# Residue-major dilated turn, gated early loads, stores on two queues and a new order in an attention + feed-forward kernel

## The chip, the cores and the metric

One core of a Trainium2 chip. The runs were spread over four chips, each beside the kernel before on the same chip. The metric is device time in microseconds (us), as the median of several executions. In every run that lists both, the time is 1.6 to 1.8 us above the span of the same execution (from the first to the last instruction), so spans of profiles are compared with spans, and times with times.

In profile lines PE is TensorE, PEld its weight loads, DVE is VectorE, ACT ScalarE, POOL GpSimd and SP SyncE; a q after the name (SPq) marks the issue of a DMA. A line of a timeline gives the start in us, the duration, engine, source line, operation, shape and count, and in brackets how long the engine stood idle before and what ended that.

## The reference

Sliding-window attention over 8 batches of 8 heads, 576 tokens, head size 64, then a feed-forward block over its output:

```python
scores = scale * np.matmul(q, k.transpose(0, 1, 3, 2))
rel = pos[:, None] - pos[None, :]
mask_plain = (rel >= 0) & (rel < window)                                  # window = 32, heads 0 to 3
mask_dil = (rel >= 0) & (rel < window * dilation) & (rel % dilation == 0) # dilation = 4, heads 4 to 7
...                                   # softmax over the allowed keys, times v
h = x @ w_in                          # 4608 x 512 @ 512 x 2048
return np.maximum(0.01 * h, h) @ w_out
```

Dilated heads only look at keys of the same residue mod 4, so each residue is a plain window of 32 over 144 tokens.

## The kernel before

The work is cut into 16 half-batches n = 0 to 15 (even: the four plain heads, odd: the four dilated ones); each has three units of scores, u = 3n + s. "Batch 5" below means half-batch n = 5. A list of steps gives the order in which instructions are issued; each engine runs its own in that order. `S` is scores and exponential, `M` the mask product, `D` the values and the normalisation, `I` one group of four matmuls into the hidden layer (hp), `O` four of the 16 into the output (op), `Z` filler matmuls without use. `B` transposes on TensorE (n below 5), `T` by DMA (n from 5 on).

```python
NPE = 5
def qk_ap(x, n, pairs):
    ...
    if n >= NPE:
        return rows_ap(x, base, [[D, 96], [96 * D, 24], [1, D]])      # 256-byte pieces
def cast_qk(n, nm, eng, pairs=(0, 1)):    # fp32 -> fp16, two pieces of 96 x 768
def transpose(n):
    for nm, dst in (("q", qT), ("k", kT)):
        o = dst[n % NB][:, -2 * S:].rearrange("p (c r) -> p c r", r=96)
        nc.sync.dma_start_transpose(o, qkh[n, nm][0:96, :])
...
# in scores(u): dilated units read every fourth column
if kind:
    ka = kT[n % NB][r, tok - 128 + j: tok - 128 + j + 4 * kp - 3: 4]
    qa = qT[n % NB][r, tok - PAD + j: tok - PAD + j + 4 * w - 3: 4]
nc.tensor.matmul(sps[0:kp, hh, w * x:w * x + w], ka, qa, ...)
...
# in values(u): the normalisation, on ACT ("l") or on VectorE ("r")
if log_recip:
    nc.scalar.activation(out=ln, in_=den[:, 0:384], func=AF.Ln)
    nc.scalar.activation(out=rec, in_=ln, func=AF.Exp, scale=-1.0)
else:
    nc.vector.reciprocal(out=rec, in_=den[:, 0:384])
...
# in ff_out(t, g): after the last four of an output tile
if g == 3:
    ob = moe.tile([128, DM], FP32, tag="ob", bufs=2, name="ob")
    nc.scalar.copy(out=ob, in_=op)
    nc.scalar.dma_start(out[128 * t:128 * t + 128, :], ob)
```

The hidden groups, the output tiles, the transposes of `B` and some of the `D` units take their PSUM from one pool of four banks; ACT empties hp and op.

The softmax here doesn't subtract the row's maximum and nothing guards it: scores larger than these inputs give would overflow.

## Time and profile before

| | before |
|---|---|
| time, median | 324.41 us (324.23 to 324.82) |
| span of the first profile | 324.1 us, of an execution of 325.84 us |
| TensorE (PE) busy | 317.0 us, 98% |
| first hp group starts | 25.39 us |
| last matmul ends | 320.57 us |

A busy PE row says only that some matmul is in flight; fillers count and durations overlap. What can be added up is the distance from the start of a group to the start of the next one. The prediction below makes a price list of such distances and adds it up along the program. Four terms then make the span: the start of the first hp group, the priced work after it, the lag (how much later PE ends than start and price say; all its small waits), and the tail from PE's end to the end of the span.

### The profile page before, as it was taken

Reading aid. Unit: us, or ns where it says so; the run is one execution under the profiler, and the core shown is the slowest. Engines: PE = TensorE matmul, PEld = TensorE weight load, DVE = VectorE, ACT = ScalarE, POOL = GpSimd, SP = SyncE. Lnnn points to the kernel's source line nnn. Section 1 sums busy time; section 2 is a strip of 40 time slices with the busy share of each in tenths; the row PEclk is TensorE's granted clock in tenths of the full one; section 3 lists DMA queues with packets and bytes.
Section 4 is the critical chain, followed back from the end, with each engine's and each line's share of the span. In section 5 each row is a group of like instructions: output and inputs, shape, how many; then the busy total and the mean of one; then the engine's idle time right before and its main releaser. Section 6 shows DMA issues by size and latency. Waiting matters only on the chain.

```text
span 324.1 us, 6641 instructions
## 1 busy us (share of the span) xinstructions
PE 317.0 (98%) x2805; PEld 185.4 (57%) x2805; DVE 111.2 (34%) x166; ACT 191.8 (59%) x379; POOL 69.3 (21%) x92
## 2 busy tenths in 40 slices
PE   8998999999999999999999999999999999999995
PEld 3565585565756656656555565555665655565542
DVE  3473363203633084012353650454561530040000
ACT  1778696555756765936755773636856754464312
POOL 8751076033054220040310610200150000000000
PEclk9999999999999999999999999999999999999999
DMA  7999999969949931579899869303755000100003
GB/s 230 209 197 196 185 180 176 164 186 106 252 79 288 205 58 48 130 161 163 116 251 245 97 115 238 85 12 117 198 67 77 34 33 28 39 34 32 32 35 129
DMA packets 111198, 42.38 MB, mean 131 GB/s; under 512 B 96832, under 2 KB 105024, under 8 KB 111168
## 3 DMA queue, kind: packets, MB, share of 16 engines
q1 hardware_dynamic: 78240, 21.83, 34.2%
q0 software_dynamic: 27744, 10.68, 28.5%
q10 hardware_dynamic: 5184, 9.44, 7.9%
q8 instruction: 22, 0.36, 0.5%
q14 instruction: 8, 0.07, 0.1%
HBM read 36.70 MB, written 9.44 MB: 142 GB/s over the span
## 4 chain that ended last, share of the span: by engine, by line
PE 88%; DMA 9%; POOL 2%; ACT 0%; issue 0%; POOLq 0%
PE op L344 39%; PE hp L334 38%; DMA w<-in_moe_w_in_dram 5%; PE sps L261 5%; DMA vh<-in_v_dram 4%; PE den L287 3%; PE o L295 2%; PE tp L212 0%; POOL vh L169 0%; POOL vh L198 0%; POOL qh L183 0%; ACT ob L348 0%; POOL bias L106 0%; POOL bias L104 0%; POOL bias L103 0%
## 5 line engine op out<-in xcount | busy, mean ns | idle before, releaser
L334 PE MATMUL hp<-xT,w 128*128 128x384 f16 (+1 forms) x832 | 140.9, 315 | 0.7 <-DMA w<-in_moe_w_in_dram 0.7
L344 PE MATMUL op<-w,gt 128*128 128x512 f16 x576 | 137.0, 379 | 0.0
L336 ACT ACTIVATE gt<-hp 128x384 f16<-128x384 f32 (+1 forms) x208 | 93.0, 465 | 66.2 <-PE hp L334 63.8
L334 PEld LDWEIGHTS <-w 128*128 128x128 f16 x832 | 88.7, 114 | 43.9 <-issue 1.6
L344 PEld LDWEIGHTS <-gt 128*128 128x128 f16 x576 | 55.1, 98 | 57.2 <-issue 0.5
L312 DVE TENSOR_TENSOR xT<-o,rec 128x384 f16<-128x384 f32 (+1 forms) x64 | 33.6, 554 | 108.0 <-ACT rec L301 90.0
L303 DVE RECIPROCAL rec<-den 128x384 f32<-128x384 f32 x14 | 35.8, 2555 | 35.3 <-PE den L287 35.3
L264 ACT ACTIVATE er<-sps 128x768 f16<-128x768 f32 (+1 forms) x48 | 38.6, 804 | 10.7 <-PE sps L261 8.8
L348 ACT COPY ob<-op 128x512 f32<-128x512 f32 x36 | 21.1, 586 | 33.6 <-PE op L344 33.5
L186 POOL CAST kh<-kf 96x768 f16<-96x768 f32 x16 | 14.6, 936 | 106.3 <-DMA kf<-in_k_dram 81.2
L271 DVE TENSOR_TENSOR em<-er,mask 128x768 f16<-128x768 f16 (+1 forms) x44 | 25.4, 600 | 18.0 <-ACT er L264 17.8
L261 PE MATMUL sps<-qT,kT 64*128 64x96 f16 (+1 forms) x448 | 22.9, 229 | 0.0
L300 ACT ACTIVATE ln<-den 128x384 f32<-128x384 f32 x34 | 16.6, 488 | 8.7 <-PE den L287 8.1
L261 PEld LDWEIGHTS <-kT 64*128 64x128 f16 (+1 forms) x448 | 14.9, 121 | 10.2 <-issue 8.6
L301 ACT ACTIVATE rec<-ln 128x384 f32<-128x384 f32 x34 | 17.8, 524 | 1.1
L295 PEld LDWEIGHTS <-vh 128*64 128x64 f16 (+1 forms) x448 | 15.5, 110 | 2.4
L295 PE MATMUL o<-em,vh 128*64 128x96 f16 (+1 forms) x416 | 15.4, 201 | 0.0
L287 PE MATMUL den<-em,ones 128*64 128x384 f16 (+1 forms) x88 | 15.4, 346 | 0.0
L387 PE MATMUL wp<-xT 128*128 128x512 f16 x37 | 12.6, 455 | 1.5 <-DVE xT L113 1.3
L174 POOL DMA_DIRECT2D vh<-in_v_dram x16 | 10.0, 627 | 18.8 <-PE o L295 18.8
L195 POOL COPY vh<-vh 32x1472 f16<-32x1472 f16 x5 | 7.0, 1404 | 24.6 <-DMA vh<-in_v_dram 24.5
L287 PEld LDWEIGHTS <-ones 128*64 128x64 f16 (+1 forms) x96 | 5.3, 107 | 10.0 <-issue 8.3
(51 smaller groups left out, 97.8 us busy)
## 6 DMA issues: line engine op xcount, KB each, us to landing
out_dram<-ob ACTq DMA_DIRECT2D x36, 256.0 KB, 2.2
qf<-in_q_dram SPq DMA_DIRECT2D x11, 576.0 KB, 6.5
kf<-in_k_dram SPq DMA_DIRECT2D x11, 576.0 KB, 7.7
vh<-in_v_dram POOLq DMA_DIRECT2D x8, 288.0 KB, 7.5
w<-in_moe_w_in_dram POOLq DMA_DIRECT2D x4, 512.0 KB, 16.1
w<-in_moe_w_out_dram POOLq DMA_DIRECT2D x4, 512.0 KB, 11.1
vh<-in_v_dram POOLq DMA_DIRECT2D x8, 192.0 KB, 5.6
qf<-in_q_dram SPq DMA_DIRECT2D x4, 288.0 KB, 5.3
```

Source lines behind the costliest of these rows:

```text
L261: nc.tensor.matmul(sps[0:kp, hh, w * x:w * x + w], ka, qa, start=not pe_mask, stop=not pe_mask or x == len(tiles) - 1)
L264: nc.scalar.activation(out=er[0:kp], in_=sps[0:kp, :, 0:384], func=AF.Exp, scale=SCALE)
L271: nc.vector.tensor_tensor(out=em[0:kp].rearrange("p h (t c) -> p h t c", c=w), in0=er[0:kp].rearrange("p h (t c) -> p h t c", c=w), in1=ba ...
L287: nc.tensor.matmul(den[64 * hh:64 * hh + 64, 0:384], ones[0:kp], em[0:kp, hh, :], start=True, stop=True)
L295: nc.tensor.matmul(o[64 * hh:64 * hh + 64, w * x:w * x + w], vt[0:kp, sl, :], em[0:kp, hh, w * x:w * x + w], start=True, stop=True)
L301: nc.scalar.activation(out=rec, in_=ln, func=AF.Exp, scale=-1.0)
L303: nc.vector.reciprocal(out=rec, in_=den[:, 0:384])
L312: nc.vector.tensor_tensor(out=out_x, in0=ins[0], in1=ins[1], op=ALU.mult)
L334: nc.tensor.matmul(hp[:, 0:w], w1[j // 4][:, i, j % 4::4], xT[:, i, x0:x0 + w], start=(i == 0), stop=(i == 3))
L336: nc.scalar.activation(out=gt[:, j, g0:g0 + w], in_=hp[:, 0:w], func=AF.Prelu, alpha=0.01)
L344: nc.tensor.matmul(op, gt[:, j, g0:g0 + 128], w2[g][:, j % 4, :], start=(j == 0), stop=(j == 15))
L348: nc.scalar.copy(out=ob, in_=op)
```

## The change

The intent: (1) order the dilated q and k by residue, so that their scores read contiguous columns; (2) keep early loads away from the start, by a one-element memset into the load's buffer on a chosen engine, for which the load must wait; (3) issue 20 of 36 stores from POOL, with 4 output buffers instead of 2, and store the last tile in two halves; (4) a new order of steps. The diff, cut to its core:

```diff
-QHB = 4
+QHB = 3
 PROGRAM: all lines replaced, for example
-... M:9 I:0:7 I:0:8 S:7:m ...  D:9:lp D:10:l lq:5:b S:14:m lv:4:b ...
+... cv:3:V:b lv:2:b I:1:2 I:1:3 I:1:4 lq:6:b:P lv:5:b O:0:0 I:1:5 I:1:6 M:11 lq:5:b:V M:9 ... O:3:3:P T:5 ...
@@ load_qk
+            if gate is not None and nm == "q":
+                gate.memset(t[0:1, 0, 0:1], 0.0)
+            if n >= NPE and n % 2:
+                for a, i0, w in ((0, 0, 96), (1, 96, 48)):
+                    nc.sync.dma_start(t[0:w, 16 * a:16 * a + 16, :]...,
+                                      rows_ap(x, ..., [[4 * D, w], [S * D, 4], [1, 4 * D]]))   # 1 KB pieces
@@ cast_qk: four pieces, 96 x 512 twice and 48 x 512 twice
@@ transpose
+            if n % 2:
+                o = t.rearrange("p (c r) -> p c r", r=144)
+                nc.sync.dma_start_transpose(o[:, :, 0:96], qkh[n, nm][0:96, 0:1024])
+                nc.sync.dma_start_transpose(o[:, :, 96:144], qkh[n, nm][0:48, 1024:2048])
@@ scores
+                if kind and n >= NPE:
+                    c = S * p + 144 * j + (96 if s == 2 else 0)
+                    ka = kT[n % NB][r, PAD + c - 32: PAD + c - 32 + kp]
+                    qa = qT[n % NB][r, c: c + w]
@@ ff_out
-            ob = moe.tile([128, DM], FP32, tag="ob", bufs=2, name="ob")
+        for c0, c1 in ((0, 256), (256, 512)) if last else ((0, 512),):
+            ...
+                ob = moe.tile([128, DM], FP32, tag="ob", bufs=4, name="ob")
+                nc.scalar.copy(out=ob[:, c0:c1], in_=op[:, c0:c1])
+                queue.dma_start(out[128 * t:128 * t + 128, c0:c1], ob[:, c0:c1])   # queue: gpsimd or scalar
```

## The prediction

> **What bounds the kernel now.** I read the page's busy totals first, then its 40 slices, then PE's waits, then the timeline of PE. Busy totals and slices of the kernel before:
>
> ```profile
> PE 317.0 (98%) x2805; PEld 185.4 (57%) x2805; DVE 111.2 (34%) x166; ACT 191.8 (59%) x379; POOL 69.3 (21%) x92
> PE   8998999999999999999999999999999999999995
> DMA  7999999969949931579899869303755000100003
> ```
>
> PE is busy from start to end; no other engine is near its limit; DMA is full only in the first third. Busy PE need not be useful PE: filler matmuls (wp) count too. The waits of PE show that little is left to be un-blocked:
>
> ```profile
> PE wp L387 <- DVE xT L113: 1.3, 1, 1.3
> PE tp L212 <- DMA kh<-in_k_dram: 0.9, 1, 0.9
> PE hp L334 <- DMA w<-in_moe_w_in_dram: 0.7, 1, 0.7
> PE tp L212 <- DVE xT L312: 0.4, 1, 0.4
> ```
>
> So the time is PE's ordered stream, and I priced it from the PE timeline as the start of a group to the start of the next (durations overlap, so they must not be added). The feed-forward matmuls go at 0.65 us for four of 384 columns (hp) and 0.86 us for four of 512 (op), plus about 0.095 us each time attention follows; 208 hp and 144 op groups make some 253 of 324 us, and the change leaves them alone. What it touches is the dilated scores:
>
> ```profile
> 237.02 0.53 PE L261 MATMUL sps<-qT,kT 64*128 64x96 f16 x8
> 248.87 0.34 PE L261 MATMUL sps<-qT,kT 64*128 64x96 f16 x8
> 257.40 0.78 PE L261 MATMUL sps<-qT,kT 64*80 64x48 f16 x16
> ```
>
> The first is a dilated unit, whose q and k are read every fourth column; the second a plain unit with contiguous columns. From start to next start the timeline gives 0.46 us against 0.275 us, the same in every such unit of the kernel; the dilated rest unit (third line, 16 matmuls) takes 0.715 us. In the windows around them the matmul itself grows from 203 to 264 ns, the weight load only from 94 to 114 ns: most of the price is in the strided moving operand.
>
> Last, the start. The timeline has the first hp group at 25.39 us. Until then PE does 11.5 us of attention work (by the prices above), the rest is 37 fillers and waits. The DMA view of the first 40 us shows why:
>
> ```profile
> q0 software_dynamic: 8776, 4.53, 81.8%
> q1 hardware_dynamic: 5792, 3.54, 40.7%
> qf<-in_q_dram SPq DMA_DIRECT2D x1, 576.0 KB, 19.6
> kf<-in_k_dram SPq DMA_DIRECT2D x1, 576.0 KB, 30.3
> ```
>
> The last two lines are the q and k of batch 5 (half-batches are numbered 0 to 15, odd ones dilated). They are issued at 7.35 and 8.26 us, as soon as two staging buffers are free, are not needed before 49 us, and hold some 30% of the engines' time in each 4 us window from 16 to 32 us, when the weights w_in must arrive. The chain that ended last runs through them: 17.3 us of DMA w, ending at 35.28 us.
>
> **What the skill says.** The Trainium skill, "TensorE: Matmul & The Clock Gate", section "Wait — 56ns, not 53.3ns?", gives N/2.4 + 2.5 ns between warm matmuls: 215.7 ns for 512 columns. The trace agrees: 0.86/4 = 215 ns, and 162.5 ns for 384. The same page, "Weight-path perf modes", has fast weight load work with 128 columns only, packed or strided; my 80-column units don't get it, so I expect less than a plain unit's speed per weight column there. "SBUF — State Buffer", section "Door 1: The DMA port swizzle", in its note on cachelines, calls strides free while two accesses hit each 16-byte line, which would make a stride of four fp16 free. The trace disagrees (0.46 against 0.275 us), and the trace decides. "DMA: Bandwidth & Descriptors", section "Specifications", asks for at least 512 B per transfer for line rate; batch 5's pieces are 256 B, and the windows agree that they are dear: about 20% of the bytes for 30% of the time.
>
> **The change, part by part.**
>
> *Residue-major dilated turn* (batches 5, 7, 9, 11, 13, 15; 1 and 3 stay strided): q and k are sorted by residue before the transpose, so the scores read contiguous columns. 12 units of 0.46 become 0.275: 12 x 0.185 = 2.2 us. 6 rest units of 0.715: the value products of the same 80x48 shape run at 0.34 us for 16, which is the least I expect; with a dearer 80-column weight load I take 0.40, so 6 x 0.315 = 1.9 us. Sum 4.1 us, wholly on PE, which never waits there, so it should come off the end. The number and width of the matmuls stay. Added: a cast of two pieces by two pairs, 4 instructions over 2048 columns for 2 over 1536 (now 936 ns each on POOL, 550 on DVE): an estimate of 0.5 to 0.8 us for each of 12 casts, some 8 us over engines with hundreds of idle us. Two DMA transposes stand for one, over the same number of elements. Loads go in pieces of 1 KB for 256 B, which takes DMA time away, but no PE wait hangs on it.
>
> *Order, counted from the program.* Before the first hp group there are now 13.5 us of attention work (batch 2's transposes and two more score units are moved up) with 35 fillers, against 11.5 with 37. Adding the fillers (0.216 us each, 2.9 us more for those that run cold, 0.1 us per change to attention) and 1.3 us of start gives 24.9 us before (measured 25.4) and 26.2 us after. With the same kind of small waits I take 26.7. The work left after that point, by the same prices, is 291.9 us before and 290.1 after without the stride gain. The 45 switches from feed-forward to attention become 43. Net of order: 1.8 gained, 1.3 given back, 0.5 us.
>
> *Gated early loads.* Batch 5's and 6's q wait for a memset on DVE or POOL, so they leave the start. The model of before has PE's last matmul at 25.4 + 291.9 = 317.3; the timeline has it at 320.6. Of these 3.2 us, 2.2 arise by 43 us, in the stretch fed by w_in and the late q, k of batches 2 and 4. I estimate the arrivals after: the bytes read by SWDGE up to the fourth w_in slice are about 7.7 MB both times, plus 2.4 MB of q and k; before, another 1.1 MB of small pieces. At the 338 GB/s that 11.2 MB by 35.3 us imply (from 2.2 us), the last slice is there near 32 us and first needed near 35. So I expect 1.0 us of stalls for 3.2: 2.2 us gained.
>
> *Stores on two queues, 4 buffers, last tile in halves.* 20 of 36 stores go to POOL. Each costs ACT 0.34 us of issue, but ACT is not the bound: nothing. The last tile is copied and stored in two halves of 256 columns, the first beside the second's matmuls; the tail is now 3.5 us (copy 0.59, issue 0.34, landing over 2): 0.3 us gained.
>
> Sum: 4.1 + 0.5 + 2.2 + 0.3 = 7.1 us, so 324.4 - 7.1 = 317.3 us, and I say **317.2**.
>
> **Rivals.** (1) *The start stays DMA-bound*: gq:3, gq:2 and both v now all stand in front of w_in on the one software queue. If w_in's slices came as late as now, the 2.2 us stay and the first hp group slips by 1 or 2 us: 320 to 321. Against it: the bytes in front are the same set, and the small pieces are gone. (2) *The fillers set the start*: 35 fillers and 13.5 us of work are a floor of 26.2 us, whatever the data do; if the data had come sooner nothing is won. That is in the number. (3) *A new wait*: POOL runs in order, and a store there makes it wait for ACT's copy of an output tile; a value copy, cast or load behind it comes late and PE stands still, with two staging buffers and three half buffers for four. For it: POOL now carries casts, copies and stores; against: POOL is 21% busy and the order was redone for it. 1 to 3 us: 318 to 320. (4) *The stride was not the cost of the rest units* (weight load of 80 columns): 1.9 us shrinks to near 0: 319.
>
> **Range and chances.** Errors of about 1 us each in the start, the stalls and the rest units, with new waits on one side only, give 314.2 to 319.8 for 8 in 10. Faster by over 2% means under 317.9 us, which lies close to my number: 0.58, within 2% 0.41, slower 0.01.
>
> **What would show it.** Dilated score units of batches 5 and up at 0.27 to 0.28 us per 8 from start to start and 0.35 to 0.45 per 16; those of 1 and 3 unchanged at 0.46 and 0.715. First hp group at 26 to 27.5 us; no load in 256 B pieces before 30 us; w_in by about 32 us; PE waits on DMA under 1 us. Value and output rates unchanged. The last output matmul to the end in about 3.2 us. The prediction is wrong if PE shows gaps after 50 us (behind POOL or DMA), if hp first runs after 28 us, or if the contiguous units don't reach the plain units' speed.

## The result, and the profile after

The changed kernel took 321.85 us (median of 4, 321.16 to 322.71) beside 324.59 us for the kernel before: ratio 0.9918, interval 0.9889 to 0.9947. A ratio is the mean time of one kernel's fast runs over that of the other's in the same rounds, so not quite the ratio of the medians. The gain is 0.8%, not 2.2%; the time lies outside the stated range. The profiled execution was the fastest of the four (321.16 us, span 319.5).

Busy totals and slices of the changed kernel: PE is as full as before; of the other engines only VectorE (111.2 to 125.5 us) and POOL (69.3 to 75.5) have gained work.

```profile
PE 312.5 (98%) x2821; PEld 184.5 (58%) x2821; DVE 125.5 (39%) x196; ACT 190.8 (60%) x375; POOL 75.5 (24%) x113
PE   8999999999999999999999999999999999999995
DMA  7999999999999829999399387391000000000102
```

The score groups in its PE timeline (start, duration, line, operation, shape, count). The first is batch 1, still strided; the next is a dilated unit of batch 5, the last its rest unit:

```profile
15.38 0.53 PE L286 MATMUL sps<-qT,kT 64*128 64x96 f16 x8
80.03 0.34 PE L286 MATMUL sps<-qT,kT 64*128 64x96 f16 x8
83.81 0.48 PE L286 MATMUL sps<-qT,kT 64*80 64x48 f16 x16
```

From start to next start these take 0.46, 0.275 and 0.42 us: the score step came out as predicted (0.275 and 0.40).

DMA in the first 40 us of the changed kernel: the hardware queue's share of the engines fell from 40.7% to 20.0%, and a w_in slice now lands 12.0 us after issue (median) instead of 16.1:

```profile
q0 software_dynamic: 7254, 6.09, 96.4%
q1 hardware_dynamic: 1525, 2.46, 20.0%
...
w<-in_moe_w_in_dram POOLq DMA_DIRECT2D x4, 512.0 KB, 12.0
```

Who PE waited for, over the whole changed kernel (us in total, times, longest). The wait for w_in is gone; waits for ACT are there instead:

```profile
PE wp L418 <- DVE xT L113: 1.3, 1, 1.3
PE hp L359 <- ACT gt L361: 1.0, 2, 0.6
PE op L374 <- ACT ob L378: 0.5, 1, 0.5
PE hp L359 <- DVE xT L337: 0.2, 1, 0.2
PE tp L233 <- DMA kh<-in_k_dram: 0.2, 1, 0.2
```

Two of those places, in the PE timeline: a hidden group just after the start, and the second half of the last output tile:

```profile
28.62 1.46 PE L359 MATMUL hp<-xT,w 128*128 128x384 f16 x8 [0.63 <-ACT gt L361]
```

```profile
314.30 1.91 PE L374 MATMUL op<-w,gt 128*128 128x256 f16 x16 [0.46 <-ACT ob L378]
```

The first waits for one of the four PSUM banks: ACT empties hp and was behind with exponentials and copies. The second is an unneeded wait that the change made itself: both halves of the last tile lie in one PSUM tile, so the second half's first matmul waits for ACT's copy of the first half.

### The profile page after: what moved, and what is told of

The parts are those of the page before. It is cut to its first block, busy times and chain, and to the rows that moved or that the text cites.

```text
span 319.5 us, 6740 instructions
## 1 busy us (share of the span) xinstructions
PE 312.5 (98%) x2821; PEld 184.5 (58%) x2821; DVE 125.5 (39%) x196; ACT 190.8 (60%) x375; POOL 75.5 (24%) x113
## 4 chain that ended last, share of the span: by engine, by line
PE 90%; ACT 4%; DMA 3%; issue 1%; POOL 0%; DVE 0%; ACTq 0%; POOLq 0%
PE hp L359 39%; PE op L374 38%; PE sps L286 4%; PE den L312 3%; DMA kh<-in_k_dram 3%; PE o L320 2%; ACT ln L325 1%; PE tp L233 1%; ACT rec L326 1%; PE wp L418 1%; ACT er L289 1%; PE sps L270 0%; ACT ob L378 0%; ACT gt L361 0%; POOL qh L169 0%
## 5 line engine op out<-in xcount | busy, mean ns | idle before, releaser
L374 PE MATMUL op<-w,gt 128*128 128x512 f16 (+1 forms) x592 | 138.9, 374 | 0.5 <-ACT ob L378 0.5
L361 ACT ACTIVATE gt<-hp 128x384 f16<-128x384 f32 (+1 forms) x208 | 94.5, 465 | 65.9 <-PE hp L359 64.9
L379 POOL DMA_DIRECT2D out_dram<-ob x20 | 11.3, 564 | 180.3 <-ACT ob L378 178.7
L378 ACT COPY ob<-op 128x512 f32<-128x512 f32 (+1 forms) x37 | 21.2, 573 | 28.3 <-PE op L374 28.2
L296 DVE TENSOR_TENSOR em<-er,mask 128x768 f16<-128x768 f16 (+1 forms) x43 | 26.8, 645 | 10.2 <-ACT er L289 10.0
L286 PE MATMUL sps<-qT,kT 64*128 64x96 f16 (+1 forms) x448 | 19.0, 209 | 0.1
L286 PEld LDWEIGHTS <-kT 64*128 64x128 f16 (+1 forms) x448 | 12.1, 106 | 10.0 <-issue 7.1
L192 POOL CAST kh<-kf 96x512 f16<-96x512 f32 (+1 forms) x12 | 7.0, 627 | 31.7 <-DMA kf<-in_k_dram 31.7
L418 PE MATMUL wp<-xT 128*128 128x512 f16 x35 | 11.7, 431 | 1.7 <-DVE xT L113 1.3
L177 POOL DMA_DIRECT2D vh<-in_v_dram x8 | 10.7, 1339 | 5.1 <-PE hp L359 2.3
L182 POOL DMA_DIRECT2D vh<-in_v_dram x16 | 10.1, 637 | 2.5 <-PE o L320 2.2
```

The costliest lines, as they stand in the source:

```text
L286: nc.tensor.matmul(sps[0:kp, hh, w * x:w * x + w], ka, qa, start=not pe_mask, stop=not pe_mask or x == len(tiles) - 1)
L296: nc.vector.tensor_tensor(out=em[0:kp].rearrange("p h (t c) -> p h t c", c=w), in0=er[0:kp].rearrange("p h (t c) -> p h t c", c=w), in1=ba ...
L361: nc.scalar.activation(out=gt[:, j, g0:g0 + w], in_=hp[:, 0:w], func=AF.Prelu, alpha=0.01)
L374: nc.tensor.matmul(op[:, c0:c1], gt[:, j, g0:g0 + 128], w2[j // 4][:, j % 4, c0:c1], start=(j == 0), stop=(j == 15))
L378: nc.scalar.copy(out=ob[:, c0:c1], in_=op[:, c0:c1])
```

## The experiments

All ran for five rounds beside the kernel before, but for e1 (three); all were correct. The four terms of each profile, in us:

| profile | first hp | priced work | lag | tail | span | ratio of times to before |
|---|---|---|---|---|---|---|
| before, first | 25.39 | 291.92 | 3.26 | 3.57 | 324.1 | |
| e1 before again | 24.70 | 291.92 | 2.30 | 3.56 | 322.5 | 0.9995 |
| after, first | 26.51 | 286.15 | 3.55 | 3.25 | 319.5 | 0.9918 |
| e4 after again | 27.12 | 286.15 | 3.22 | 3.24 | 319.7 | 0.9916 |
| e2 turn only, old order | 25.39 | 287.93 | 3.33 | 3.57 | 320.2 | 0.9968 |
| e15 same, 4 output buffers | 24.72 | 287.93 | 2.54 | 3.56 | 318.7 | 0.9893 |
| e5 changed code, old order | 28.19 (clock fell) | 287.93 | 4.36 | 3.49 | 324.0 (slow) | 0.9869 |
| e3 gate only | 25.20 | 291.92 | 1.56 | 3.55 | 322.2 | 0.9976 |
| e6 strided, new order | 26.81 | 290.14 | 3.13 | 3.26 | 323.3 | 1.0031 |
| e7 new order, no gates | 29.93 (clock fell) | 286.15 | 4.99 | 3.23 | 324.3 | 1.0017 |
| e8 new order, ACT stores | 28.89 | 286.15 | 6.84 | 3.49 | 325.4 | 1.0009 |
| e9 7 fewer fillers | 28.79 (clock fell) | 286.15 | 3.47 | 3.23 | 321.6 | 0.9932 |
| e10 tail in two PSUM tiles | 27.91 | 286.15 | 2.61 | 3.25 | 319.9 | 0.9912 |
| e11 old order, that tail | 24.84 | 287.93 | 2.73 | 3.48 | 319.0 | 0.9901 |
| e12 old order, that tail, gate | 23.86 | 287.93 | 2.10 | 3.49 | 317.4 | 0.9849 |
| e16 e12 again | 24.64 | 287.93 | 2.82 | 3.48 | 318.9 | 0.9882 |
| e13 two reciprocals on VectorE | 28.44 | 286.15 | 5.57 | 3.24 | 323.4 | 1.0002 |
| e14 one reciprocal on ACT | 28.95 (clock fell) | 286.15 | 2.33 | 3.23 | 320.7 | 0.9909 |
| e17 ACT cluster spread | 27.83 | 286.34 | 2.54 | 3.25 | 320.0 | 0.9901 |

Half-widths of the 95% intervals are 0.0017 to 0.0030 for most, 0.0034 to 0.0042 for e2, e8, e9, e11 and e15. "Clock fell" means that TensorE's granted clock was at half for a while; in an execution's mean clock over the whole span such a fall shows as 0.995 or less. The profile of one execution need not show what the median does; first hp alone varies by 0.6 to 1.4 us between executions of one kernel.

### e1 and e4: the two kernels again

No edit. 

> The kernel before, unchanged, profiled again. The first profile of it came from an execution of 325.84 us, while its timed executions took 324.23 to 324.82 us; it held 2.1 us of lag of TensorE against the price list between 29.3 and 36.1 us (waits for w_in and for k of batch 4). Theory A (the lag there varies from run to run and that execution was a slow one): this profile has a span near 322.7 us and a lag there of about 0.7 us. Rival B (the profile is typical and only the profiler's own cost differs): span again 324.1 us and lag again 2.1 us.

> The changed kernel, profiled and timed again. If the variation of its executions (321.2 to 322.7 us) is in the small waits of hp and op for ACT, this profile has a total lag of 3.5 us or more against the price list when its time is above 321.2 us, spread over waits for ACT after 50 us. Rival: it is in the start, before the first hp group at 26.5 us. Ratio 0.992 as before.

The kernel before had a span of 322.5 us and a lag of 0.8 us at 34 us, where the first profile had 2.1. PE's wait for w_in in e1:

```profile
PE hp L334 <- DMA w<-in_moe_w_in_dram: 0.6, 2, 0.4
```

So theory A holds: the profile that the prediction was built on came from an execution 1.4 us slower than the timed ones. Of the 1.6 us of span between the two profiles, 0.7 lie in the start and 1.0 in the lag, in the very waits that the gates were to take away: for w_in and for k of batch 2 (the text says batch 4, but the transposes that waited are those of batch 2). In e4, at 321.44 us, the lag was 3.2 us, not over the 3.5 us named; the start was 0.6 us later than in the first profile of after. What varies between executions is more the start than the lag.

### e2, e15, e5: the turn in the old order

e2 is the changed code with the old order's steps and

```diff
-        last = t == NTOK // 128 - 1
+        last = False
-                ob = moe.tile([128, DM], FP32, tag="ob", bufs=4, name="ob")
+                ob = moe.tile([128, DM], FP32, tag="ob", bufs=2, name="ob")
```

> Only the residue-major turn (loads, casts, transposes, scores) for batches 5 to 15 odd, in the old order, all stores on ACT, last tile whole, no gates; the half buffers are 3 instead of 4 for room. Theory: 12 units at 0.275 for 0.46 us and 6 at 0.42 for 0.715 us come wholly off the end: 4.0 us, ratio 0.988, and TensorE's lag against the price list stays near 3 us. Rival: the longer casts or the third missing half buffer bring waits of TensorE that give 1 us or more back: 0.991 or worse.

It gave 1.8 us of 4.0 between the medians, and still less by the ratio (one of its six executions took 325.83 us). Two of the six, 325.83 and 323.91 us, ran with a fallen clock (mean 0.995). Its ACT timeline, then its PE timeline, show where one us went:

```profile
67.00 0.58 ACT L378 COPY ob<-op 128x512 f32<-128x512 f32 x1 [3.69 <-DMA out_dram<-ob]
```

```profile
67.64 3.67 PE L359 MATMUL hp<-xT,w 128*128 128x384 f16 x20 [0.96 <-ACT ob L378]
```

A store held one of two output buffers for so long that ACT stood still for 3.7 us, and hp behind it for 1 us. e15 puts the second diff line back (4 buffers); e5 puts both back.

> As e2 (contiguous turn alone, old order) but with 4 output buffers for 2; no gate, stores on ACT, last tile whole. e2 stood at 0.9968 with a wait of 0.96 us of hp behind a store that held one of two buffers; e5 and e11, with 4 buffers and the last tile in halves, at 0.987 and 0.990. Theory: the buffers are what lets the score gain through: 0.989 to 0.991. Rival: e2 was slow for another cause (its start), and this stays at 0.996.

> The changed code (residue-major turn, 4 output buffers, last tile in halves) run in the old order: no gates, all stores on ACT. The contiguous turn alone had a wait of 0.96 us of hp on ACT at 67 us, behind a copy that waited 3.7 us for a store to free one of 2 output buffers. Theory: with 4 buffers that wait is gone and the score gain shows more fully: 3 to 3.7 us, ratio 0.989 to 0.991, so that the new order and the gates add nothing to it. Rival: other waits of the same kind take its place and it stays at 0.995 to 0.997, and the new order is what turns the score gain into time.

0.9893 and 0.9869: 3.4 to 4.0 us. With 4 buffers the score gain shows nearly in full, without the new order, without gates, with all stores on ACT. That supports the buffers as the cause in e2; the intervals of e2 and e15 just touch, so the size stays rough. Without the executions with a fallen clock (two in e2, two in e15, one in e5) the plain means are 0.9934, 0.9871 and 0.9868 of before, so some 2 us lie between 2 and 4 buffers. e5's profiled execution was a slow one (325.67 us, wait of 2.0 us for v, then a fall of the clock) and is not used for its terms.

### e3: the gate alone

```diff
-... D:10:l lq:5:b S:14:m ...
+... M:9 lq:5:b:V I:0:7 ...        (and the gate argument of load_qk)
```

> The kernel before with one change: the q load of batch 5 waits for a memset on VectorE placed after the mask product of unit 9, so that it starts near 35 us instead of 7. Theory of the prediction: the w_in slices come earlier and the 2.2 us of lag before 43 us go: ratio 0.993. Rival (the lag of a typical run is well under 2 us there, as the profiled run of before was a slow one): 0.5 to 1 us, ratio 0.997 to 0.9985.

0.9976, 0.8 us (0.2 to 1.4 by the interval): the rival. The waits for w_in did go (lag 1.56), but a typical execution had only about 0.8 us of them.

### e6: the strided turn in the new order

```diff
-            if n >= NPE and n % 2:        # load, cast, transpose
+            if False:
-                if kind and n >= NPE:     # scores
+                if False:
```

> The changed kernel with the old strided form of the dilated turn (256-byte loads, one transpose each, two-piece casts, scores at stride 4) and all else as changed. If the 4.0 us of PE price are worth their full size in the new order: 325.6 us, ratio 1.004 to the kernel before. If part of it was only waiting turned elsewhere, less: 324 us. The 8-matmul units of batches 5 and up go back to 0.46 us, the 16-matmul ones to 0.715.

1.0031 against 0.992: 1.15%, 3.7 us. The priced work differs by 4.0 us. So the turn is worth what its price says. e6 took back its loads, casts and transposes too, but PE's lag (3.13 us, for 3.55 and 3.22 with the turn) did not move with them, so the gain lies in the score matmuls. Everything else in the change together costs 1.0 us against the kernel before (the interval of e6: 0.3 to 1.7 us).

### e7 and e8: what the gates and the POOL stores are worth in the new order

```diff
e7: lq:6:b:P, lq:5:b:V, lq:14:b:V  ->  lq:6:b, lq:5:b, lq:14:b
e8: nc.gpsimd if len(a) > 2 else nc.scalar  ->  nc.scalar
```

> The changed kernel without the three gating memsets. The first early load (q and k of batch 6, 256-byte pieces) is then issued near 7 us. Theory: it takes DMA time from w_in and the late q, k of batch 2; either hp waits for w_in (0.5 to 1.5 us, as before) or the first hp group comes later; ratio 0.994 to 0.996. Rival: the fillers and ACT set the start and the weights have slack: no change, 0.9916.

> The changed kernel with all stores issued from ACT again. 20 issues of 0.34 us come back to ACT. Prediction's reading (ACT is not the bound): no change, 0.9916. Rival: ACT's lateness is what hp waits for now (about 2 us of lag of the profile), so the stores on ACT make it longer by 0.5 to 1.5 us: 0.993 to 0.996.

Both lose the whole gain. In e7 five of the six executions ran with a fallen clock, but the sixth, at 326.12 us, was no faster. In its profile w_in landed 19.3 us after issue (median) and PE waited for data behind the early load:

```profile
PE op L374 <- DMA w<-in_moe_w_out_dram: 1.9, 1, 1.9
...
PE o L320 <- POOL vh L210: 1.2, 1, 1.2
```

In e8, ACT's timeline, SP's, and PE's at the same time, and what ACT waited for from 96 to 103 us:

```profile
96.86 0.59 ACT L378 COPY ob<-op 128x512 f32<-128x512 f32 x1
101.07 0.34 ACTq L379 DMA_DIRECT2D out_dram<-ob  x1
101.46 1.09 ACT L361 ACTIVATE gt<-hp 128x192 f16<-128x192 f32 x3 [4.01 <-DMA kf<-in_k_dram]
```

```profile
90.82 0.44 SPq L156 DMA_DIRECT2D kf<-in_k_dram  x1
...
96.55 5.28 SPq L221 DMA_TRANSPOSE kT<-kh  x1
```

```profile
101.84 0.81 PE L359 MATMUL hp<-xT,w 128*128 128x384 f16 x4 [1.66 <-ACT gt L361]
```

```profile
ACT gt L361 <- DMA kf<-in_k_dram: 4.0, 1, 4.0
```

ACT's copy ended at 97.45, but its store was issued only at 101.07. ACT ran nothing meanwhile; PE lost 2.6 us of lag there. What held the store was a load of k: SP had issued it at 90.82, it landed at 101.00, and the store's wait ended at 101.02. In the trace both report their landing to the same completion semaphore (number 109). In this program the DMAs of SP and ACT take eight such semaphores in turn, those of POOL eight others, and here the store had to wait until the load in front of it on that semaphore was done. SP was also busy issuing a DMA transpose at the time, which looks like the cause and is not: the store went out before that ended, and in e5 another store on ACT was issued 0.03 us after its copy in the middle of a long transpose:

```profile
107.93 3.74 SPq L224 DMA_TRANSPOSE kT<-kh  x1
```

```profile
108.71 0.59 ACT L378 COPY ob<-op 128x512 f32<-128x512 f32 x1 [1.24 <-PE op L374]
109.33 0.34 ACTq L379 DMA_DIRECT2D out_dram<-ob  x1
```

A late store of this kind happened once in 37 stores of e8, and in no other profile. The Trainium skill, "DMA: Bandwidth & Descriptors", section "Issuing engines are not separate DMA queues", calls the time to initiate a DMA usually small; the 0.34 us of a store on ACT, beside some 2 us to its landing, agrees, and the 3.62 us were a wait and not issue time. A store on POOL is outside SP's and ACT's eight semaphores and does not hold ACT up. So e8's reading is: the POOL stores are worth some 3 us in the new order (interval wide, 0.9973 to 1.0045), and the old order does without them (e5 and e15 have all stores on ACT). The larger part of e8's profiled loss (5.7 us of span against e4, in one of its two slowest executions) is elsewhere, 1.8 us of it in a later start, and is not explained.

### e9: fewer fillers

```diff
-... D:3:rp Z:2 cv:0:P:b Z:1 mask lw:1:0 S:1:b Z:3 D:0:lp S:11:m Z:1 D:1:lp ...
+... D:3:rp cv:0:P:b mask lw:1:0 S:1:b D:0:lp S:11:m D:1:lp ...
```

> The changed kernel with 7 of the 35 filler matmuls taken out, those between unit 3's values and unit 1's values, shortly before the first hp group. Theory (rival 2 of the prediction: the fillers set the first hp group, not data): hp starts 1.5 to 1.9 us earlier, near 25 us, and the time falls by 1 to 1.9 us, ratio 0.986 to 0.989. Rival: ACT's and VectorE's chains (exponentials, copies of transposes, normalisation) or w_in set it; waits of the same size appear where the fillers were, ratio 0.9916.

Neither. PE's granted clock, by window (us, length, busy us and count of PE, PEld, DVE, ACT, POOL, then the clock, the DMA share and GB/s):

```profile
26.00:28.00 2.00, 2.00 (x72) 1.78 (x72) 1.89 (x3) 1.28 (x3) 0.53 (x1) 0.71 1.25 211
28.00:30.00 2.00, 2.00 (x28) 1.17 (x24) 1.53 (x4) 1.71 (x3) 1.28 (x2) 0.50 1.32 197
30.00:32.00 2.00, 2.00 (x13) 1.28 (x11) 0.94 (x3) 1.32 (x3) 0.34 (x1) 0.93 1.25 218
```

Worked out from these windows, the clock was at half for about 3.4 us (0.29 + 0.50 + 0.07, each over 0.5 and times 2 us). e5, e7 and e14 show the same 3.4 us at half speed in their starts. e9's two executions at a mean clock of 1.0 took 320.97 and 321.14 us, the other four (0.984 to 0.995) 321.61 to 325.05; all six of e10, with all fillers, on the same chip, had 1.0 and took 321.81 on average. So the fillers seem to do two things: they take PE time that is partly free anyway (waits of 0.4 to 0.6 us for VectorE and ACT came in their place, and the two undisturbed executions gained 0.75 of the 1.5 us taken out), and they keep the clock up.

### e10 and e11: the tail, in both orders

```diff
         for c0, c1 in ((0, 256), (256, 512)) if last else ((0, 512),):
+            if c0:
+                op = psm.tile([128, 512], FP32, tag="pm", name="op")
```

> The changed kernel with the second half of the last output tile in a PSUM tile of its own. Theory: the 0.46 us that op waits for ACT's copy of the first half (both halves lie in one PSUM tile) go, so the last store is issued 0.4 to 0.5 us earlier: ratio 0.990. Rival: the last matmuls are not what the end waits for: 0.9916.

> The changed code in the old order (as e5, 0.9869) with the second half of the last tile in its own PSUM tile. Theory: e5 less 0.4 us, ratio 0.9855 to 0.987, that is 1.0 to 1.8 us under the changed kernel, so the new order with its gates and POOL stores is worth less than nothing here. Rival: e5's figure was luck of its 4 fast runs and this is at 0.990 or above, level with e10.

The 0.46 us wait went (lag 2.6), but the time, 0.9912, is not told apart from 0.9916: at most half of it shows. e11 at 0.9901 does not tell the orders apart either; one of its six executions (324.35 us) had a fallen clock.

### e12 and e16: the old order with one gate

e11 with e3's move of batch 5's load.

> As e11 with the early load of batch 5 gated as in e3 (which alone gave 0.9976). Theory: w_in comes earlier and the waits for it in the old order go: 0.5 to 0.8 us under e11, ratio 0.983 to 0.985. Rival: batch 5's load, now in 1 KB pieces, no longer hurts w_in, so the gate gives nothing: same as e11.

> The same kernel as e12, again, beside the others on one chip: old order, contiguous turn, 4 buffers, batch 5's load gated, last tile in halves in two PSUM tiles. Theory: 0.985 as before, 4.5 to 5 us under the kernel before and 1.5 to 2 us under the new order. Rival: 0.990, e12 was luck.

0.9849 and 0.9882, the best: 319.92 and 320.98 us. In e12 PE waits for nothing that matters after its first 1.3 us:

```profile
PE wp L420 <- DVE xT L113: 1.3, 1, 1.3
PE hp L359 <- ACT gt L361: 0.2, 1, 0.2
```

On the same chip, e12 is 1.8 us under the new order with the same tail (e10, 321.76 us), with intervals apart. In the second call the gap to e14 was 0.8 us and the intervals overlap. So the old order with one gate is at least as good as the new order, probably a little better.

The gate also goes with a steady clock. In the old order with the turn and without a gate, 6 of 23 executions (e2, e15, e5, e11) ran with a fallen clock; with the gate none of 12 did (e12, e16), and none of the 43 of the kernel before whose clock is listed. In e5's profile PE's wait before the fall was for a v that landed at 17.3 us, after the first piece of batch 5's q (15.6 us), which nothing needed yet. So the prediction's "no PE wait hangs on it", said of the loads in 1 KB pieces, does not hold for a load that is not gated; how the wait comes about is read from that one profile.

### e13, e14, e17: what holds the new order up

```diff
e13: D:34:lp -> D:34:rp, D:46:lp -> D:46:rp       (on e10)
e14: D:3:rp -> D:3:lp                             (on e10)
e17: D:34:lp cq:14:k:V:b D:29:l S:31:m O:16:0 M:31 cq:12:k:V:b I:7:8 I:7:9
  -> D:34:lp cq:14:k:V:b S:31:m O:16:0 M:31 cq:12:k:V:b I:7:8 I:7:9 D:29:l    (on e10)
```

> The changed kernel with the tail of e10, and the normalisation of units 34 and 46 by VectorE's reciprocal instead of two ACT instructions. Theory: the steps of lag at unit 33 (0.6 to 0.8 us) and unit 44 (0.25 to 0.5 us) are hp waiting for an ACT that is late with its evictions after a cluster of log, exponential and score exponential; with 1 us less on ACT in front of each they shrink below 0.2 us and the time falls by 0.5 to 1 us, ratio 0.988 to 0.9897. Rival: VectorE's 2.56 us reciprocal delays masks and xT by as much: no change, 0.9912.

> The changed kernel with the tail of e10, and unit 3's normalisation, in the start, on ACT instead of VectorE's 2.56 us reciprocal. VectorE was busy for 5.7 of 6 us from 20 to 26 us in e9. Theory: VectorE's chain helps set the first hp group, so it comes 0.5 to 1 us earlier than in e10 (27.9 us) and e4 (27.1), at 26.3 to 26.8, next to the floor of 26.2 us that work and fillers set; ratio 0.988 to 0.990. Rival: the fillers hold it anyway, 0.9912, or ACT is then late: worse.

> The changed kernel with the tail of e10 and one move in its order: unit 29's values and its two ACT normalisation steps come after the first two hp groups that follow, instead of before unit 31's scores. The amount of work on each engine is the same; only the cluster on ACT is spread. Theory: the step of TensorE's lag at unit 33 (0.6 to 0.8 us in the changed kernel, e4, e6, e7, e9, e10) falls to 0.2 us or less and the lag at the end by 0.5 us, ratio 0.9895; in time that is at the edge of what 5 rounds resolve, so the lag in the profile is what counts. Rival: that step has another cause (e13, which moved the work to VectorE, made it worse): it stays at 0.6 us or more.

e13 was worse by 3 us, and shows its rival at work: the reciprocal held VectorE, masks and normalisations came late, and PE waited for them.

```profile
178.64 2.55 DVE L328 RECIPROCAL rec<-den 128x384 f32<-128x384 f32 x1
...
185.56 0.35 PE L312 MATMUL den<-em,ones 128*64 128x384 f16 x2 [1.28 <-DVE em L296]
```

e14 was level with e10 (0.9909); its profiled execution had a fallen clock after a wait of 1.5 us for k of batch 3, so its profile does not tell what sets the start; its five other executions took 321.62 us on average, for 321.81 in e10. e17 does tell something: the step of lag at unit 33, 0.6 to 0.8 us in after, e4, e6, e9 and e10, fell to 0.2 us. So that step was the cluster of ACT work. But a step of 0.3 us came up at unit 40 (under 0.12 in e10), the switches added 0.2 us of price, and PE ended no earlier.

## Why the prediction was wrong, point by point

Predicted: span 324.1 - 7.1 = 317.0, time 317.2. Measured: span 319.5 in the profile, median time 321.85. The miss of 4.65 us is made of 2.5 us in the span of the profile, 1.4 us because the profile that the prediction subtracted from came from a slow execution (325.84 us, for a median of 324.41), and 0.7 us because the profiled execution of the changed kernel was a fast one. In the prediction's own terms the first hp group came at 26.51 us for 26.7, the priced work was 286.15 us for 286.0, the tail 3.25 us for 3.2, and the lag 3.55 us for 1.0: the 2.5 us of span are the lag alone.

- **Score step: right in size.** 4.1 us predicted, 4.0 by the price list, 3.7 in time (e6). The stride was the cost; no run separates the moving operand from the weights. In the units of 8 mostly the matmul had grown, as predicted; in the rest units the weight load gained more by the turn (mean 166 to 117 ns, from 60 us on) than the matmul (232 to 195 ns). At 117 ns for 80 columns it is still dearer than a plain one (94 ns for 128), as expected; the units came to 0.42 us.
- **"The model of before has PE's last matmul at 317.3; the timeline has it at 320.6 ... I expect 1.0 us of stalls for 3.2: 2.2 us gained": this step failed.** The lag of the changed kernel is 3.55 and 3.22 us. The old waits did go as predicted: the last slice of w_in landed at 30.5 and 31.7 us (predicted 32) and PE no longer waited for it. But new waits took their place, which the number had left out: rival 3 in kind, but behind ACT and VectorE and not behind POOL, 0.3 to 0.6 us after the start, about 0.4 at 57 to 60 us behind xT, 0.6 to 0.8 near 180, about 0.3 near 256, 0.46 in the tail. And the gain was not there in full: the waits for w_in and k of batch 2 were 2.1 us in that one profile and 0.8 in e1, and the gate alone gave 0.8 us (e3). The profile's own execution time, 325.84 us beside a median of 324.41, was overlooked.
- **Order: "1.8 gained, 1.3 given back".** The first hp group came at 26.51, as predicted, and at 27.12 in e4; the mean is 1.8 us later than the two profiles of before, so all is given back. What sets it is left open: the fillers' floor of 26.2 us would explain most, but half the fillers' time came back as waits in e9, and the profiles of e9 and e14 were spoiled by the clock.
- **Stores on two queues: "ACT is not the bound: nothing".** Wrong as a reading. ACT's busy share is not the question; a store that has to wait for a slow load of SP on the same semaphore stops ACT. The new order needs the POOL stores (e8), as it needs the gates (e7). The 4 buffers, which the prediction gave nothing, are what lets the score gain through in the old order (e2, e15).
- **Tail: 0.3 us gained** from PE's end to the end, as predicted (3.57 to 3.25), less the 0.46 us wait between the halves. But the reason given was only part of it: the halves alone, with all stores on ACT, gained under 0.1 us (3.49 in e5 and e8); the rest shows only where earlier stores go by POOL, and is not explained.
- **Range.** It allowed new waits of 1 to 3 us but counted the base as known; the profile was one draw from executions that spread over 2 us.

Where did the expected gain go? The turn's 3.7 us arrived. The gates' gain was mostly not there to be had, the order's 1.8 us were given back in the start, and new waits behind ACT and VectorE of some 2.5 us, 0.5 of it in the tail, took the place of the old ones. The gates and the POOL stores are needed there to keep it from losing more (e7, e8).

## What to carry to other kernels

Compare the time of the profiled execution with the timed ones before reading any wait as typical, and profile twice where the step depends on a wait of 1 or 2 us. On a saturated engine a price list by start-to-start distance predicts a change of its own instructions to a few tenths of a us; waits around it need an experiment each. Where something starts late, look at the releaser that the trace names before what happened to run at the same time (e8). When several parts are changed together, try the one that acts on the bound alone with the buffers it needs: here the turn with four buffers, one gate and the old order was as good as the whole change or better.

## What the Trainium skill lacked or had wrong

- "SBUF — State Buffer", section "Door 1: The DMA port swizzle", note on cachelines: strides that still hit each 16-byte line twice are called free. Score matmuls with both operands at a stride of 8 bytes took 0.46 us for 8 from start to start, 0.275 us contiguous; the rest units 0.715 and 0.42 us.
- "TensorE: Matmul & The Clock Gate", section "Part 1: The HAM clock gate": its table puts the fall to half clock after at least one idle window of about 3.4 us. Here it fell after far shorter waits: from 10 us on, the longest wait of PE before the fall was 0.6 us in e9, 1.2 in e7, 1.5 in e14 and 2.0 in e5. In e9 PE was still busy for 1.30 to 1.52 of each 2 us from 20 to 26 us. A later section of the page does have frequent short idle times bring the clock down, without a figure for how short. That the clock stays at half for one window of about 3.4 us agrees in all four.
- "DMA: Bandwidth & Descriptors", section "Issuing engines are not separate DMA queues": it gives sequencer time as all that issuing from several engines saves. In e8 the engine also decided whom a store waited for: on ACT it shared a completion semaphore with a load of SP and was issued 3.62 us after its copy, when that load had landed. Stores on POOL use other semaphores. How semaphores are shared is a matter of the program as built.
- "TensorEngine Tiling (Array Packing)", section "Key Properties", says that a change of tiling mode drains TensorE, and gives no price. What fits it here is 0.095 us more each time a feed-forward group is followed by an attention group (0.96 for 0.86 us, 0.74 for 0.65 us), and 0.10 us more when value products are followed by scores or a feed-forward group than when they are followed by the next unit's softmax sums (den), whose weights have the same 128x64 shape (0.27 for 0.17 us). No run shows that the drain is what costs this.
